# Routed experts at fitted widths, window attention in steps of two blocks, scores in bands of keys

## The chip, the core and the metric

The kernel runs on one NeuronCore of a Trainium2 chip. Its engines work side by side, each through its own queue in order: TensorE (PE; its weight loads are listed as PEld), VectorE (DVE), ScalarE (ACT), GpSimd (POOL) and SyncE (SP, which here only issues DMAs). The metric is the device time of one execution in microseconds; less is better.

## The reference

Two blocks follow each other, in float32. The first is attention with a local window and a few global keys: batch 4, 8 heads, 768 positions, head size 64.

```python
scores = scale * np.matmul(q, k.transpose(0, 1, 3, 2))
is_global = pos[None, :] < int(n_global)                 # n_global = 8
is_local = (rel >= 0) & (rel < int(n_local))             # n_local = 96
bias = -slopes[:, None, None] * dist[None, :, :]         # dist: distance, or n_local for a far global key
a = softmax(np.where(is_global | is_local, scores + bias, -1e9))
x = (a @ v) as 3072 tokens of 512 numbers                # heads side by side
```

The second sends each token to one of 8 experts (512 to 1024 to 512), the one whose embedding has the largest cosine with it, and weighs the result with that expert's probability.

```python
expert_idx = np.argmax(xn @ en.T / tau, axis=1)
for e in range(E):
    mask = expert_idx == e
    h = np.maximum(x[mask] @ w1[e], 0.0)
    out[mask] = gate_w[mask, None] * (h @ w2[e])
```

## The kernel before

Attention works on 8 groups (a batch and four of its heads, as two pairs `a` of two heads `e`). In a group the keys are cut into 8 blocks of 96; a unit is one block of keys with the 192 queries that can see it (the last: 96), and 30 rows of global keys ride along, so a score tile has 126 partitions. `score` (L329) multiplies keys by queries for four heads into two PSUM banks, takes one exponential of both banks on ACT (L341), and multiplies with a table of decays and masks on DVE (L347). `attend` (L349) runs one unit behind: v products (L367), and products with a matrix of ones that give the softmax denominators (L373), into three of four banks `od`; after four blocks they are copied to `xd`. Between them PE turns the next group's k and q (`turn`, L315) and works off one task of a list: `sums` (L398; logits of a tile of 128 tokens with the expert embeddings, L405, and transposes of denominators and of the last tile's logits) or `rows` (L425; transposes x, scales it, writes it to DRAM). `finish` calls `choose` (L145): the best expert, a token's rank within it by a matmul with a triangular matrix, its gate, and one small scatter for each tile of 128 tokens, which writes token number and gate to the expert's slots in DRAM (`meta`). The order of instructions on an engine is the scheduler's, from the order of the program.

The table (`window_table`, L236) is made at the start, from position tiles that POOL writes and numbers that are loaded by DMA.

The experts follow. `load_rows` (L626) reads 512 slots of an expert (it waits for all scatters), gathers their rows of x with four indirect DMAs; unused slots point at a row of zeros. `expert` (L648) transposes them (L655, copied by DVE, L656), takes the first product (L664: eight blocks of 128 hidden units, 512 columns of tokens), relu on ACT (L666), the second product (L671: four tiles of 128 tokens, 512 columns), scales by the gate (L674) and scatters rows to the output (L675). Every expert has 512 slots, however many tokens it has. Weights of the next expert load meanwhile into the other of two buffers. `leftover` (L681) handles what doesn't fit, behind a branch that isn't taken here (L699, L700).

## Time and profile before

| | us |
|---|---|
| median of three runs | 768.54 (766.0 to 772.91) |
| the profiled execution | 777.63 |
| its span, first to last instruction | 775.8 |
| PE busy in the span | 686.5 (88%) |
| DVE, ACT, POOL busy | 182.4, 147.6, 112.6 |
| granted PE clock, mean | 0.95 |

Busy times say how long an engine had an instruction in it; matmuls overlap, so a busy PE need not be a fast one. The granted clock is given as a share of 2.4 GHz; its two levels here are 1.0 and 0.5.

### The profile page before, as it was taken

Reading aid. Unit: us, or ns where it says so; the run is one execution under the profiler, and the core shown is the slowest. Engines: PE = TensorE matmul, PEld = TensorE weight load, DVE = VectorE, ACT = ScalarE, POOL = GpSimd, SP = SyncE. Lnnn points to the kernel's source line nnn. Section 1 sums busy time; section 2 is a strip of 40 time slices with the busy share of each in tenths; the row PEclk is TensorE's granted clock in tenths of the full one; section 3 lists DMA queues with packets and bytes.
Section 4 is the critical chain, followed back from the end, with each engine's and each line's share of the span. In section 5 each row is a group of like instructions: output and inputs, shape, how many; then the busy total and the mean of one; then the engine's idle time right before and its main releaser. Section 6 shows DMA issues by size and latency. Waiting matters only on the chain.

```text
span 775.8 us, 8382 instructions
## 1 busy us (share of the span) xinstructions
PE 686.5 (88%) x3394; PEld 353.0 (46%) x3394; DVE 182.4 (24%) x500; ACT 147.6 (19%) x280; POOL 112.6 (15%) x131
## 2 busy tenths in 40 slices
PE   4989986989799519999999999999999999999992
PEld 2556654555465304444444444444444444444440
DVE  2435562664366601011011011011011011011010
ACT  3545532543453200100100100100100100100100
POOL 2110022013003232012012012012012011010010
PEclk9999989898999758999999999999999999999996
DMA  9977669650110922214214115115114114000000
GB/s 185 213 129 213 177 177 39 137 118 7 37 42 16 283 48 90 83 58 174 81 53 171 78 71 175 71 64 172 64 70 168 64 77 146 0 37 14 0 26 18
DMA packets 99898, 74.57 MB, mean 96 GB/s; under 512 B 80762, under 2 KB 80890, under 8 KB 99850
## 3 DMA queue, kind: packets, MB, share of 16 engines
q1 hardware_dynamic: 90538, 58.44, 29.8%
q0 software_dynamic: 5888, 14.71, 5.4%
q10 hardware_dynamic: 3424, 0.79, 0.6%
q8 instruction: 29, 0.48, 0.3%
q14 instruction: 19, 0.16, 0.1%
HBM read 61.11 MB, written 14.90 MB: 98 GB/s over the span
## 4 chain that ended last, share of the span: by engine, by line
PE 59%; DVE 4%; DMA 3%; issue 0%; POOL 0%; SPq 0%; ACT 0%; DVEq 0%; ACTq 0%
PE big L664 29%; PE work L671 28%; DVE xT L656 2%; DMA x_dram<-xs 1%; DMA xg<-x_dram,ids 1%; DMA meta<-mt,slot 1%; DVE y L674 1%; PE tp L405 0%; PE tp L430 0%; PE tp L408 0%; DMA emt<-meta 0%; PE od L367 0%; PE work L655 0%; POOL out_dram L675 0%; SPq L630 0%
## 5 line engine op out<-in xcount | busy, mean ns | idle before, releaser
L664 PE MATMUL big<-xT,w1t 128*128 128x512 f32 x512 | 224.0, 598 | 11.2 <-DVE xT L656 11.2
L671 PE MATMUL work<-w2t,hT 128*128 128x512 f32 x512 | 221.0, 592 | 0.0
L664 PEld LDWEIGHTS big<-xT,w1t 128*128 128x128 f32 x512 | 97.4, 192 | 133.2 <-issue 120.0
L671 PEld LDWEIGHTS work<-w2t,hT 128*128 128x128 f32 x512 | 97.3, 190 | 122.5 <-issue 122.5
L674 DVE TENSOR_SCALAR y<-work,emt 128x512 f32<-128x512 f32 x32 | 24.0, 751 | 387.2 <-PE work L671 387.2
L666 ACT ACTIVATE hT<-big 128x1024 f32<-128x1024 f32 x32 | 32.8, 1023 | 432.0 <-PE big L664 432.0
L347 DVE TENSOR_TENSOR ex<-ex,table 126x384 f32<-126x384 f32 (+1 forms) x128 | 70.1, 585 | 89.0 <-ACT ex L341 89.0
L675 POOL DMA_INDIRECT out_dram<-y,ids x32 | 31.8, 995 | 337.8 <-DVE y L674 330.1
L337 PE MATMUL sp<-qT,kT 64*126 64x192 f32 (+1 forms) x512 | 66.8, 364 | 7.9 <-ACT qT L325 5.8
L367 PE MATMUL od<-ex,v 126*64 126x192 f32 (+1 forms) x576 | 62.6, 320 | 8.6 <-issue 4.6
L341 ACT ACTIVATE ex<-sp 126x768 f32<-126x768 f32 x64 | 49.1, 767 | 82.6 <-PE sp L337 60.8
L337 PEld LDWEIGHTS sp<-qT,kT 64*126 64x126 f32 x512 | 43.9, 196 | 28.1 <-issue 13.1
L367 PEld LDWEIGHTS od<-ex,v 126*64 126x64 f32 x576 | 34.1, 138 | 28.5 <-issue 18.6
L640 POOL DMA_INDIRECT xg<-x_dram,ids x32 | 30.9, 966 | 85.4 <-issue 42.9
L373 PE MATMUL od<-ex,ones 126*32 126x192 f32 (+1 forms) x576 | 36.3, 321 | 0.0
L655 PE MATMUL work<-ident,xg 128*128 128x128 f32 x128 | 17.7, 293 | 18.9 <-DMA xg<-x_dram,ids 18.9
L199 POOL DMA_INDIRECT meta<-mt,slot x24 | 23.8, 993 | 44.1 <-DVE slot L190 30.3
L655 PEld LDWEIGHTS work<-ident,xg 128*128 128x128 f32 x128 | 15.5, 151 | 23.7 <-DMA xg<-x_dram,ids 20.1
L320 PE MATMUL tp<-ident,k 128*128 128x128 f32 x96 | 19.7, 329 | 6.3 <-DMA k<-in_k_dram 6.0
L311 POOL COPY v<-v 30x1792 f32<-30x1792 f32 x8 | 13.6, 1698 | 74.8 <-DMA v<-in_v_dram 46.6
L430 PE MATMUL tp<-ident,xd 128*128 128x128 f32 x96 | 16.3, 298 | 8.2 <-DVE lh L420 6.3
L656 DVE COPY xT<-work 128x512 f32<-128x512 f32 x32 | 20.1, 682 | 6.8 <-PE work L655 6.5
(113 smaller groups left out, 297.4 us busy)
## 6 DMA issues: line engine op xcount, KB each, us to landing
w1t<-in_moe_w_dram SPq DMA_DIRECT2D x8, 2048.0 KB, 7.9
w2t<-in_moe_w_dram SPq DMA_DIRECT2D x8, 2048.0 KB, 10.8
k<-in_k_dram SPq DMA_DIRECT2D x32, 192.0 KB, 3.5
v<-in_v_dram SPq DMA_DIRECT2D x32, 192.0 KB, 4.5
x_dram<-xs SPq DMA_DIRECT2D x24, 256.0 KB, 6.3
q<-in_q_dram SPq DMA_DIRECT2D x28, 192.0 KB, 3.9
q<-in_q_dram ACTq DMA_DIRECT2D x4, 192.0 KB, 6.1
xg<-x_dram,ids POOLq DMA_INDIRECT x32
```

The source lines that it names most:

```text
L337: nc.tensor.matmul(sp[0:ROWS, e, a * n : (a + 1) * n], lhsT=t.kT[rows, j, 0:ROWS], rhs=t.qT[rows, j * BLK : j * BLK + n], start=True, stop ...
L341: nc.scalar.activation(ex, sp[0:ROWS, :, 0 : 2 * n], AF.Exp, scale=k.scale)
L347: nc.vector.tensor_tensor(out=exv, in0=exv, in1=tb, op=ALU.mult)
L367: nc.tensor.matmul(od[a][e * D : (e + 1) * D, cols], lhsT=g.v[0:ROWS, 2 * a + e, j, :], rhs=ex[:, e, a * n + c0 : a * n + c1], start=first ...
L373: nc.tensor.matmul(od[2][32 * i : 32 * i + 32, cols], lhsT=k.ones[0:ROWS, 0:32], rhs=ex[:, e, a * n + c0 : a * n + c1], start=first, stop= ...
L655: nc.tensor.transpose(ps[:, c, :], xgs[j][:, c * P : (c + 1) * P], k.ident[:])
L656: nc.vector.tensor_copy(out=xT[:, :, j * P : (j + 1) * P], in_=ps[:])
L664: nc.tensor.matmul(ps[:, i, :], lhsT=w1[:, c, f * P : (f + 1) * P], rhs=xT[:, c, :], start=c == 0, stop=c == k.NC - 1)
L666: nc.scalar.activation(hT[:, 2 * f2 : 2 * f2 + 2, :], ps[:], AF.Relu)
L671: nc.tensor.matmul(ps[:], lhsT=hT[:, f, j * P : (j + 1) * P], rhs=w2[:, f, :], start=f == 0, stop=f == k.NF - 1)
L674: nc.vector.tensor_scalar_mul(y[:], ps[:], mt[:, j, 1:2])
L675: nc.gpsimd.indirect_dma_start(out=k.out[:, :], out_offset=bass.IndirectOffsetOnAxis(ap=ids[:, j : j + 1], axis=0), in_=y[:], in_offset=No ...
```

## The change

In attention, a step is two units. Both units' scores come first on PE, then k and q of the next group, transposes of finished halves, and the v and ones products of the step before. Scores are computed in bands of 32 keys, each with the 128 queries that its keys can see, in 32-column strips of the array (`bands`); the exponential is taken for each bank (`grow`), the table multiplied once for a unit (`weigh`). PSUM is five rotating banks and three for `od`. Denominators of a batch's two groups are put in different columns by `halves` and added on DVE, so that they are turned once. Logits and their transposes are done for three tiles at once. The last two groups are interleaved by halves. The order on PE, ACT, DVE and SP is the program's (a manual schedule). Scatters of slots are held back and issued one or two in a step.

At the start, loads are split in halves in the order of use, the copies of global rows of group 0 come by DMA, an exponential loads ACT's table early, PE gets a few matmuls without use, and the table is made in two parts. Weights are loaded in 32 pieces an expert, in attention too, for experts 0 and 1.

Expert 0's first 256 slots, filled by the first three batches, are gathered three steps before the end (`first_rows`); their first product stands behind the last attention product, among the last router's work.

Each expert has a jump table of 13 arms, one for each width from 128 to 512 tokens in steps of 32 (`WIDTHS`). Only PE and ACT jump; the index comes from the counts (`choose_widths`). An arm holds the first product at that width, the whole tiles of 128 tokens of the second but the first, a left-over of 64 or 32 tokens in strips (`part_in_arm`), and the transposes of the next expert's rows. The jump's target is announced ahead (`switch_hint`), then a tile of the second product that every width has is done outside. Scatters of all tiles are issued in any case; those that a width lacks get row numbers out of range.

```diff
+WIDTHS = [128] + list(range(160, CAP + 1, 32))
...
+    for t in range(n):
+        nc.tensor.matmul(cp[:, (t + 1) * E : w + E], lhsT=k.ones[:],
+                         rhs=oh[:, t : t + 1, :].to_broadcast([P, n - t, E]), start=False, stop=True,
+                         skip_group_check=True)
...
     for m in range(2):
+        yield
...
+        bands = [(i * BAND, (i + 1) * BAND, i * BAND, min(i * BAND + BAND + BLK, n)) for i in range(BLK // BAND)]
+        bands.append((BLK, ROWS, 0, BLK))
...
+            for k0, k1, c0, c1 in bands:
+                for e in range(2):
+                    rows = slice(e * D, (e + 1) * D)
+                    nc.tensor.matmul(u.sp[e][k0:k1, a * n + c0 : a * n + c1], lhsT=t.kT[rows, j, k0:k1],
+                                     rhs=t.qT[rows, j * BLK + c0 : j * BLK + c1], start=True, stop=True,
+                                     skip_group_check=True)
...
+    def grow(u, e):
+        nc.scalar.activation(u.ex[:, e], u.sp[e][0:ROWS, 0 : 2 * u.n].rearrange("p (a c) -> p a c", a=2), AF.Exp,
+                             scale=k.scale)
+    def weigh(u):
+        kind = min(u.j, 2)
+        tab = k.table[0:ROWS, u.g.m].rearrange("p e a i c -> p (e a) i c")[:, :, kind::(3 - kind), :]
+        exv = u.ex.rearrange("p e a (i c) -> p (e a) i c", c=BLK)
+        nc.vector.tensor_tensor(out=exv, in0=exv, in1=tab[:, :, 0 : u.n // BLK, :], op=ALU.mult)
...
+    def attend(g, p):
+        if p % 2 == 0:
+            g.od = [po_p.tile([P, 512], F32, name="od%d" % i, tag="od%d" % i) for i in range(3)]
+        parts = []
+        if p == 2:
+            parts.append((g.units[3], 0, BLK, 2 * BLK, True))
+        for j in (2 * p, 2 * p + 1):
+            parts.append((g.units[j], (j % QB) * BLK, 0, BLK if j % QB == QB - 1 else 2 * BLK, j == 0))
...
+        if p % 2:
+            xd = xd_p.tile([P, 2, QB * BLK], F32, name="xd", tag="xd")
+            nc.scalar.copy(out=xd[:, 1, :], in_=g.od[1][:, 0 : QB * BLK])
+            nc.vector.tensor_copy(out=xd[:, 0, :], in_=g.od[0][:, 0 : QB * BLK])
+            g.xd.append(xd)
+            h, den = p // 2, g.batch.den
+            if g.m == 0:
+                den[h] = den_p.tile([P, QB * BLK], F32, name="den", tag="den")
+                nc.vector.tensor_copy(out=den[h][:], in_=g.od[2][:, 0 : QB * BLK])
+            else:
+                nc.vector.tensor_tensor(out=den[h][:], in0=g.od[2][:, 0 : QB * BLK], in1=den[h][:], op=ALU.add)
...
+    def turn_sums(hf):
+        t, h = hf.t, hf.h
         ps = bank()
+        for c in range(3):
+            nc.tensor.transpose(ps[:, c * P : (c + 1) * P], t.den[h][:, c * P : (c + 1) * P], k.ident[:])
...
+        for a in range(4):
+            nc.tensor.matmul(ps[32 * a : 32 * a + 32, 0 : 3 * P], lhsT=k.enb[:, a, :],
+                             rhs=t.groups[a // 2].xd[h][:, a % 2, :], start=True, stop=True)
...
+    def first_rows():
+        k.first = Net()
+        k.first.rows = load_rows(k, k.meta[0:FIRST, :], k.ea, k.ea2, FIRST // P, nc.gpsimd, k.ZR + 1)
...
+    def first_product(f):
+        if f % 2 == 0:
+            k.first.ps = bank()
+        ps = k.first.ps
+        for c in range(k.NC):
+            nc.tensor.matmul(ps[:, (f % 2) * FIRST : (f % 2 + 1) * FIRST], lhsT=k.w[0][0][:, c, f * P : (f + 1) * P],
+                             rhs=k.first.xT[:, c, :], start=c == 0, stop=c == k.NC - 1)
+        if f % 2:
+            nc.scalar.activation(k.first.hT[:, f - 1 : f + 1, :], ps[:].rearrange("p (i n) -> p i n", i=2), AF.Relu)
...
+    steps = [(g, p) for g in groups[: 2 * B - 2] for p in range(4)]
+    steps += [(g, p) for h in range(2) for g in groups[2 * B - 2 :] for p in (2 * h, 2 * h + 1)]
...
+    for s, (g, p) in enumerate(steps):
...
+        for u in us:
             score(u)
...
+        grow(us[0], 0)
+        grow(us[0], 1)
+        if s == 0:
+            next(table)
+        weigh(us[0])
+        scatter_later(k, 1 if s < len(steps) - 8 else 2)
+        grow(us[1], 0)
+        todo = [(x.pairs[a], i) for x, a, i in turns[s]]
+        if todo:
+            turn(*todo.pop(0))
+        grow(us[1], 1)
+        for x in todo:
+            turn(*x)
...
+        if s > 0:
+            q, qp = steps[s - 1]
+            attend(q, qp)
...
+        if s == len(steps) - 3:
+            scatter_later(k, len(k.later))
+            first_rows()
...
+    attend(*steps[-1])
+    for hf in active:
+        half_turns(hf)
+        half_router(hf)
+    scatter_later(k, len(k.later))
+    hf = start_half(t, 1)
+    score_experts(hf, bank())
+    first_turn()
+    turn_sums(hf)
+    xs = [turn_x(t, 3)]
+    turn_products(hf)
+    next(hf.router)
+    xs += [turn_x(t, 4), turn_x(t, 5)]
+    for i in range(3):
+        store_x(t, 3 + i, xs[i])
+    weights_part(len(weights))
+    first_product(0)
+    hf.router.send(bank()[:, 3 * P :])
+    next(hf.router)
+    next(hf.router)
+    scatter_later(k, len(k.later))
+    check_sums(t)
+    first_product(1)
+    for f in range(2, k.NF):
+        first_product(f)
...
+    mt = gp.tile([P, NJ, 3], F32, name="emt", tag="emt")
+    i = nc.sync.dma_start(mt[:], slots.rearrange("(j p) w -> p j w", p=P))
...
+def part_in_arm(k, t, hT, w2, base, size):
+    nc, n = k.nc, P // size
+    m = k.DM // n
+    ps = k.work.tile([P, k.DM], F32, name="work", tag="work")
+    for f in range(k.NF):
+        for i in range(n):
+            nc.tensor.matmul(ps[i * size : (i + 1) * size, 0:m], lhsT=hT[:, f, base : base + size],
+                             rhs=w2[:, f, i * m : (i + 1) * m], start=f == 0, stop=f == k.NF - 1)
+    nc.scalar.mul(t.y_part[size][:], ps[:, 0:m], t.parts[size][1][:])
...
+def first_by_eight(k, xT, w1, hT, w, between=None):
+    nc = k.nc
+    for f in range(k.NF):
+        ps = k.big.tile([P, CAP], F32, name="big", tag="big")
         for c in range(k.NC):
+            nc.tensor.matmul(ps[:, 0:w], lhsT=w1[:, c, f * P : (f + 1) * P], rhs=xT[:, c, 0:w],
+                             start=c == 0, stop=c == k.NC - 1)
+        nc.scalar.activation(hT[:, f, 0:w], ps[:, 0:w], AF.Relu)
+        if between:
+            between(f)
...
+    def between(f):
+        for j in {5: (0,), 6: (1, 2), 7: (3,)}.get(f, ()) if coming else ():
+            turn_row(k, coming.rows, coming.xT, j, k.nc.scalar.copy)
+    tiles = range(0 if behind else 1, CAP // P)
+    for arm in tc.Switch(now.width.index, len(WIDTHS), hint=now.width.hint):
+        w = WIDTHS[arm]
+        first_by_eight(k, now.xT, w1, hT, w, between)
+        for size in (64, 32):
+            if w % (2 * size) >= size:
+                part_in_arm(k, now, hT, w2, w // (2 * size) * 2 * size, size)
+        for j in tiles:
+            if j < w // P:
+                second_in_arm(k, now, hT, w2, j)
+    if coming:
+        coming.width = take_width(k, coming.e)
+    def scatters():
+        for j in tiles:
+            scatter_rows(k, now.y[:, j, :], now.tile_ids[:, j : j + 1])
+        for size in (64, 32):
+            scatter_rows(k, now.y_part[size][:], now.parts[size][0][:], P // size)
+    out = [scatters]
+    if behind:
+        behind(out)
+    else:
+        second(k, now.rows, hT, w2, 0, k.work0, out)
...
+    v = k.nc.values_load(k.pick[0:1, e : e + 1], engines=ARMS, min_val=0, max_val=len(WIDTHS) - 1)
+    t.index, t.hint = {eng: v for eng in ARMS}, "expert%d" % e
+    k.tc.switch_hint(t.index, len(WIDTHS), t.hint)
...
+            choose_widths(n)
+            coming = numbers(0)
+            prepare(coming)
+            coming.width = take_width(n, 0)
+            second(n, n.first.rows, n.first.hT, n.w[0][1], 0, n.work)
...
+            for e in range(n.E):
+                now, coming, after = coming, after, None
+                if coming:
+                    prepare(coming)
+                for scatter in pending:
+                    scatter()
+                if e + 2 < n.E:
+                    after = numbers(e + 2)
+                    split_rows(n, after)
+                behind = None
+                if e == 0:
+                    def behind(out):
+                        second(n, n.first.rows, n.first.hT, n.w[0][1], 1, n.work0, out)
+                pending = expert(n, now, coming, behind)
```

## Rows read from the trace of the kernel before

**Rows 1.** The page: busy tenths of PE in 40 equal slices of the span.

```profile
PE   4989986989799519999999999999999999999992
```

**Rows 2.** Windows by stage: us; busy PE, PEld, DVE, ACT, POOL; PEclk; DMA; GB/s.

```profile
0.00:21.30 21.30, 8.07 (x28) 5.42 (x28) 5.23 (x20) 8.55 (x19) 5.63 (x22) 1.00 1.07 188
21.30:254.30 233.00, 209.14 (x2162) 130.70 (x2162) 120.87 (x340) 102.84 (x219) 36.32 (x37) 0.94 0.55 108
254.30:294.06 39.76, 13.28 (x73) 9.17 (x66) 14.25 (x73) 3.44 (x12) 14.86 (x17) 0.58 0.55 171
294.06:760.50 466.44, 456.00 (x1138) 207.73 (x1138) 40.91 (x65) 32.75 (x32) 54.76 (x56) 1.00 0.23 82
760.50:775.80 15.30, 0.05 (x1) 0.00 (x0) 1.17 (x4) 0.00 (x0) 0.98 (x1) 0.57 0.06 18
```

**Rows 3.** Chain of waits, expert 1 and its next: start us, us, what.

```profile
354.61 27.73 PE big L664 x64
382.34 27.48 PE work L671 x64
...
413.05 27.73 PE big L664 x64
```

**Rows 4.** Timeline of PE, one steady unit: start us, us, instructions.

```profile
211.92 0.43 PE L405 MATMUL tp<-xd,enb 128*32 128x128 f32 x8
212.27 0.44 PE L408 MATMUL tp<-ident,xd 128*128 128x128 f32 x2
...
212.75 0.87 PE L367 MATMUL od<-ex,v 126*64 126x192 f32 x8
213.55 0.53 PE L373 MATMUL od<-ex,ones 126*32 126x192 f32 x8
214.01 0.92 PE L337 MATMUL sp<-qT,kT 64*126 64x192 f32 x8
214.86 0.55 PE L320 MATMUL tp<-ident,k 128*128 128x128 f32 x3
215.25 0.60 PE L430 MATMUL tp<-ident,xd 128*128 128x128 f32 x4
215.78 0.55 PE L367 MATMUL od<-ex,v 126*64 126x96 f32 x8
```

**Rows 5.** PE's waits in attention: for whom, us, times, longest.

```profile
PE tp L430 <- DVE lh L420: 6.3, 1, 6.3
...
PE od L367 <- issue: 4.6, 3, 4.0
```

**Rows 6.** Windows around an idle stretch of PE, columns as in rows 2.

```profile
42.20:45.40 3.20, 0.30 (x9) 0.09 (x9) 1.53 (x4) 1.09 (x3) 0.99 (x3) 1.00 0.31 71
45.70:49.20 3.50, 3.50 (x17) 2.65 (x15) 0.19 (x1) 2.21 (x5) 2.09 (x3) 0.51 0.44 101
```

**Rows 7.** Timeline of the start, PE and ACT.

```profile
5.96 1.51 PE L320 MATMUL tp<-ident,k 128*128 128x128 f32 x6 [5.96 <-DMA k<-in_k_dram]
...
17.49 3.41 ACT L274 ACTIVATE table<-rel 128x384 f32<-128x384 f32 x8 [3.85 <-DVE rel L270]
...
21.32 1.01 PE L337 MATMUL sp<-qT,kT 64*126 64x192 f32 x4 [5.78 <-ACT qT L325]
```

**Rows 8.** Groups by shape, exponentials on ACT: busy us, mean ns, idle before.

```profile
L341 ACT ACTIVATE ex<-sp 126x768 f32<-126x768 f32 x56 | 45.3, 808 | 74.5 <-PE sp L337 58.3 <-remote 8.2 <-issue 3.3
...
L341 ACT ACTIVATE ex<-sp 126x384 f32<-126x384 f32 x8 | 3.8, 477 | 8.1 <-remote 5.6 <-PE sp L337 2.5
```

**Rows 9.** Chain of waits, the hole before the experts.

```profile
275.59 6.05 DMA meta<-mt,slot
...
284.91 6.25 DMA xg<-x_dram,ids x2
```

**Rows 10.** L699 and L700, PE sequencer: ns least/median/most, starts us.

```profile
L699 PEldq TENSOR_LOAD <-fi x1: 492/492/492, 761.8 to 761.8; - x1
...
L700 PEldq COMPARE_BRANCH  x1: 4402/4402/4402, 762.4 to 762.4; - x1
```

More of the change, by code (lines that the diff above doesn't have):

```diff
@@ L41, in build_consts @@
     nc.vector.memset(k.ones[:], 1.0)
+    k.halves = pool.tile([P, 2, 2, 16], F32, name="halves")
+    nc.vector.memset(k.halves[:], 0.0)
+    for m in range(2):
+        nc.vector.memset(k.halves[:, m, m, :], 1.0)
 def build_route_consts(k):
@@ L208, in choose, with scatter_later @@
             k.scatters.append(i.ins)
+    k.later.extend((scatter, t) for t in range(n))
+    if k.scatters is None:
+        scatter_later(k, n)
+    yield
+def scatter_later(k, n):
+    for scatter, t in k.later[:n]:
+        scatter(t)
+    del k.later[:n]
 def route(k, b, xb, pool):
@@ L369, in attend @@
                                      skip_group_check=True)
+        for u, at, c0, c1, first in parts:
             for a in range(2):
@@ L460, in window_attention @@
+    groups = [new_group(b, m) for b in range(B) for m in range(2)]
     for g in groups:
+        g.units = []
         for j in range(NB):
@@ L463, in window_attention @@
             u.g, u.j, u.n = g, j, (2 * BLK if j < NB - 1 else BLK)
[L464 to L477 removed]
+            u.late = g.b == B - 1 and j == QB - 1
@@ new lines, in window_attention @@
+            g.units.append(u)
+    first = groups[0]
+    open_group(first)
+    numbers = load_numbers(k, k.n_global, k.n_local)
+    build_consts(k)
+    for a in range(2):
+        load_tokens(nc.sync, first.pairs[a].k, k.k, 0, a, 0, 3)
+        load_tokens(nc.scalar, first.pairs[a].q, k.q, 0, a, 0, 3)
+    next(numbers)
+    warm = const.tile([P, 1], F32, name="warm")
+    nc.scalar.activation(warm[:], k.ones[:, 0:1], AF.Exp)
+    for a in range(2):
+        load_tokens(nc.sync, first.pairs[a].q, k.q, 0, a, 3, NT)
@@ new lines, in window_attention, with busy @@
+    for a in range(2):
+        load_tokens(nc.sync, first.pairs[a].k, k.k, 0, a, 3, NT)
+    for ps in banks:
+        nc.vector.memset(ps[:], 0.0)
+    idle = bank()
+    def busy(n):
+        for _ in range(n):
+            nc.tensor.matmul(idle[:, 0:64], lhsT=k.ones[:], rhs=k.ones[:, 0:64], start=True, stop=True)
+    busy(8)
+    load_v(first, range(4))
+    emb = prep_expert_emb(k, k.emb_in, k.tau, tmp)
+    next(emb)
+    open_group(groups[1])
+    for p in range(4):
+        load_part(groups[1], p)
@@ L518, in window_attention @@
-    while tasks:
-        tasks.pop(0)()
+    table = window_table(k, tmp)
+    next(table)
+    next(numbers)
+    next(table)
+    check_numbers(k)
+    build_route_consts(k)
+    steps = [(g, p) for g in groups[: 2 * B - 2] for p in range(4)]
+    steps += [(g, p) for h in range(2) for g in groups[2 * B - 2 :] for p in (2 * h, 2 * h + 1)]
+    turns = [[] for _ in steps]
+    turn(first.pairs[0], 0)
+    turn(first.pairs[0], 2)
+    busy(3)
+    turn(first.pairs[1], 0)
+    turn(first.pairs[1], 2)
@@ new lines, in expert @@
+def expert(k, now, coming=None, behind=None):
+    tc = k.tc
+    w1, w2 = now.w
+    hT = k.hp.tile([P, k.NF, CAP], F32, name="hT", tag="hT")
+    if coming:
+        coming.xT = k.xtp.tile([P, k.NC, CAP], F32, name="xT", tag="xT")
+    def between(f):
[21 more added lines that the diff above has]
+        behind(out)
+    else:
+        second(k, now.rows, hT, w2, 0, k.work0, out)
+    return out
```

758 lines of the change are left out of this document (476 added, 282 removed).

## The prediction, made before the change was run

> **What bounds the kernel now.** I read the page's strip of forty slices first: TensorE (PE) reads 9 in nearly all of them, with one hole between 250 and 300 us and a smaller one at the start [rows 1]. A busy PE is a share, not a limit, so next come the windows cut at four events: first steady score, last attention product, first expert matmul, last expert matmul [rows 2]. They give five stages: start 21.3 us, attention 233.0, a hole of 39.8 between attention and experts, experts 466.4, drain 15.3. In the expert stage the chain of waits is PE alone: 64 matmuls of the first product take 27.73 us, 64 of the second 27.48, and the next expert begins 58.44 us after the last, so 3.2 us go to transposes and their copies [rows 3]. That stage is bound by columns streamed: every expert is padded to 512 tokens. In the hole the chain is DMA latency and routing arithmetic, with PE mostly idle. Attention needs the order of PE in one steady unit [rows 4].
>
> **What one unit costs on PE.** Start to start in [rows 4]: expert logits (8 instructions of 128 columns, four column strips) 0.35 us, v products (8 of 192 columns, two strips) 0.80, ones products (8 of 192, four strips) 0.46, scores (8 of 192, two row halves) 0.85, three transposes 0.39, four 0.53. An f32 matmul is two instructions here. Strips run side by side: v is four rounds, ones two, and their difference, 0.34 us, is two rounds of 192 columns; so a round is 0.17 us (0.113 for 128 columns) and each change of strip pattern costs about 0.12 (0.17 for scores). The logits check this: 2 x 0.113 + 0.12 = 0.35. A unit is 0.85 + 0.80 + 0.46 + 0.39 = 2.50; 64 units are 160 us, and 24 token tiles with logits, sums and x rows at about 1.4 bring it to some 199 with routing. The stage took 233. The other 34 are PE idle in the list of PE's waits (its longest are DVE's logits, 6.3, and "issue", 4.6 [rows 5]) and half clock: 0.94 granted over 233 us [rows 2] is 28 us at 1.2 GHz, and [rows 6] show how it comes: PE nearly idle from 42.2 to 45.4, then the clock at 0.51 for the next 3.5 us though PE was busy throughout.
>
> **Start: 21.3 to about 9 us.** The first score waited for a copy queued on ScalarE (ACT) behind eight table exponentials, which ran from 17.49 [rows 7]. Those waited for position tiles that GpSimd (POOL) made behind a copy of v. The change sends group 0's global rows by DMA, loads halves in the order of need, makes the position tiles first and cuts the table in two, its first half after the first exponential. The first three-tile halves are 0.79 MB; at the stage's 188 GB/s [rows 2] that is 4.2 us; the first transposes run at 5.96 now [rows 7], and twelve of them with their copies end near 9. The DMA share there is already 1.07 [rows 2], so groups 0 and 1 (4.7 MB and the broadcast) are in by about 27 us and steps 1 to 3 wait some 6 us; that is in the stalls below.
>
> **Attention: 233 to about 185 us.** A step has two units. Scores in bands: three bands of 32 keys see 128 queries each (a key needs only its 96 and its band), the global rows 96, in 32-column strips and two row halves. That is 64 instructions for a step instead of 16. Eight strips side by side make 8 rounds of 0.113 + 0.17 = 1.08 us, against 1.70 now. No row shows eight together; rows show two and four [rows 4]. I take eight, since both patterns pack fully; the far bounds are four together, 16 x 0.113 + 0.17 = 1.98, and the logits' 0.044 us an instruction as if issue were the limit, 2.8. v products of two units follow each other without a change of pattern: 8 x 0.17 + 0.12 = 1.48; ones 4 x 0.17 + 0.12 = 0.80; six transposes 0.78. A step is 4.14, 32 are 132. For each half batch 18 transposes (sums of both groups are added first, so three, not six) at 0.13 and logits of 384 columns (2 x 0.34 + 0.12) make 3.1, eight are 25; six routers with one ones-matmul a tile, about 8. Sum 165. To it come 20 us of stalls: the start's 6, and 14 of the 34 now. The lag of a whole step between weighing and attending takes away waits such as the 6.3 us one; code fetch may grow, since 24 matmuls and as many weight loads a unit, 3,000 instructions, are added on PE and "issue" waits are there already. Bounds 8 to 40.
>
> ACT and VectorE (DVE) don't take over: ACT was busy 102.8 us here, DVE 120.9 [rows 2]. An exponential per bank costs 2 x 0.477 for 0.808 [rows 8], so ACT gains 64 x 0.15 = 9 us, to 112. DVE's two multiplies become one. Both stay far under 165. What is queued on PE behind a late exponential is a whole step, so such a wait would show at once.
>
> **The hole: 39.8 to about 34 us.** The chain now is routing, the last scatter's landing (6.05, at 281.6), the slots' reading (gathers start at 284.9), gathers (6.25 for two) [rows 9], transposes. The change leaves each link and shortens the front: three token tiles remain after the last product instead of up to six, one chain of logits. Step by step (copies 0.6, logits 0.8, copy 0.5, transposes, DVE sums 0.8, choice 1.1, x rows 2.1, squares, power, slots) I get the slots at +11 us, the last scatter issued at +15, landed at +21, slots read at +24, gathers and copies done at +34. Slots are read as 512 pieces of 12 bytes instead of 128 of 32: up to a microsecond more, counted. Under this cover PE does expert 0's first 256 rows, gathered three steps earlier: 64 instructions of 256 columns, 13.9 us, and one tile of the second product, 6.87. If the cover went, those 21 us would stand in the expert stage. POOL's queue holds the first half's three scatters ahead; it was busy 14.9 of the 39.8 us [rows 2], so they are out before the slots come. Bounds 28 and 40.
>
> **Experts: 466.4 to about 341 us.** The reference's own routing of its seeded inputs sends 406, 310, 510, 319, 322, 369, 472 and 364 tokens; 315 of expert 0's come in the first three batches, so 256 are taken early and 150 remain. Rounded up, the widths are 160, 320, 512, 320, 352, 384, 480, 384, together 2,912 columns instead of 4,096. First product: 27.73 x 2912 / 512 = 157.7. Second: 20 whole tiles in the widths and expert 0's second early tile, 21 x 6.87 = 144.3. Left-over strips: 64 rows four times, 32 instructions of 256 columns in two strips, 16 x 0.227 + 0.12 = 3.75, 15.0 together; 32 rows three times, 16 x 0.113 + 0.12 = 1.93, 5.8 together. If strips didn't overlap they would cost 7.3 and 7.2 each, 30 us more. Transposes of the coming expert now stand inside the arm: 28 x 4 x 0.13 = 14.6, with no wait for DVE. Each expert adds a register load (0.49 [rows 10]) and a jump in and out on PE and ACT. The only jump that the trace has, at the end, held PE's sequencer for 4.40 us [rows 10]. Here the target is announced before 6.87 us of outside matmuls that are already queued, so I take 0.5 a jump pair and keep 8.8 as the bound. POOL's ten indirect DMAs an expert, 0.98 us each now (54.8 for 56 [rows 2]), lie under 26 to 57 us of matmuls, and weights of 4 MB likewise. Sum 157.7 + 144.3 + 20.8 + 14.6 + 4 = 341.4.
>
> **Drain** as now, 15.3: five scatters of the last arm go out beside the outside tile.
>
> **Sum against the profiled execution.** 9 + 185.5 + 34 + 341.4 + 15.3 = 585.2 against a span of 775.8; 1.8 lies around the span, 587. The profiled execution of 777.63 stands 1.2% above the median of 768.54; the same ratio gives 580.
>
> The Trainium skill, "Runtime: NRT & Kernel Launch", Instruction fetch mechanics, says that a taken branch whose target is outside what is loaded waits for its code to come by DMA. By that rule the arms would cost what the second rival says; the trace agrees with it at the final jump (4.40 us) and shows no announced one.
>
> **Rivals.**
> Bands pack only four wide, or are limited by issue: for it, no row with eight. It gives 32 x 0.9 = 29 us more, 609; by the logits' pace 32 x 1.7 = 55, 635. Chance 0.20. The Trainium skill, "TensorE: Matmul & The Clock Gate", Wait — 56ns, not 53.3ns?, gives a floor of about 25 ns from one matmul's start to the next; an estimate by it is 64 x 0.025 = 1.6 us a step, 597 in all, while rows go no lower than 44 ns.
> Jumps are not covered: 16 x 4.4 = 70 us, 650. For it the final jump, against it the announced target and the queue ahead of it. Chance 0.08.
> Slower: each break at an arm leaves PE at 1.2 GHz, as after the idle in [rows 6], and the whole expert stage stays there. Its 337 us of streaming then double, 913. It turns the sign once over 56% of them, (768.5 - 580) / 337, run at half clock. Against it: 1.00 over all eight experts now [rows 2], with a 3.2 us gap at each. Chance 0.01.
> The change doesn't do what it says, every expert picks 512: 124 us more, 704. The counts speak against it. Chance 0.01.
> Better than summed: eight strips pack, stalls fall to 8, the hole to 28: 560 or a little under. Chance 0.12.
> Forecast: 0.58.
>
> **Range and chances.** The low end, 550, is the last case with a shorter start; the high end, 640, takes in narrow bands and half the jump loss. A change under 1% can't be told from none here. All cases but one lie far below: faster 0.97, within 1% 0.01, slower 0.02.
>
> **What would show it.** First steady score near 9 us; 32 steps near 5.5 us with eight score instructions starting within one round; last attention product near 195; first arm's matmuls near 229; PE gaps under 1 us at the jumps; outside-tile-to-outside-tile times that follow the widths, from 27 us (expert 0) to about 57 (expert 2); last matmul near 570. The sum is wrong if PE waits for ACT in each step, if the granted clock falls in the arms, or if PE's code comes late.

## The result, and the profile after

The changed kernel takes 593.1 us at the median of four runs (584.05 to 595.8) beside 769.87 for the kernel before (766.0 to 772.91): ratio 0.7644, 95% interval 0.7579 to 0.771. The ratio is not that of the two medians (0.7704): of the four runs it leaves out the two that lie over 1.5% above the fastest, 594.41 and 595.8, and takes in two more, 587.35 and 590.24. Forecast were 580, range 550 to 640. A second series of six runs gave 587.78 (584.86 to 593.75), ratio 0.7619 (0.7582 to 0.7656); the experiments are compared with that one. The profiled execution took 584.05 us, its span 582.1.

The page's strip of forty slices for TensorE in the changed kernel, to be laid beside [rows 1]:

```profile
PE   8889999999898978999999999999999999999920
```

The hole in the middle is gone from this strip, and at its end two slices are nearly empty where it was one. The same five windows as in [rows 2], same columns, changed kernel:

```profile
0.00:11.00 11.00, 8.51 (x40) 8.39 (x40) 6.28 (x24) 3.98 (x8) 4.16 (x28) 1.00 0.77 161
11.00:184.40 173.40, 161.95 (x3623) 124.24 (x3626) 110.04 (x253) 106.43 (x281) 46.30 (x49) 0.96 0.83 176
184.40:219.70 35.30, 29.26 (x139) 21.02 (x132) 13.26 (x61) 6.43 (x15) 11.75 (x12) 0.94 0.53 132
219.70:556.72 337.02, 336.07 (x1280) 184.46 (x1281) 40.18 (x204) 57.33 (x112) 71.28 (x73) 1.00 0.34 116
556.72:582.10 25.38, 0.28 (x3) 0.19 (x1) 1.20 (x4) 0.00 (x0) 3.91 (x4) 0.57 0.05 14
```

| stage, us | before | forecast | after |
|---|---|---|---|
| start | 21.3 | 9 | 11.0 |
| attention | 233.0 | 185.5 | 173.4 |
| hole | 39.8 | 34 | 35.3 |
| experts | 466.4 | 341.4 | 337.0 |
| drain | 15.3 | 15.3 | 25.4 |
| span | 775.8 | 585.2 | 582.1 |

The experts give two thirds of the gain, attention nearly a third. The drain, the stretch behind the last expert matmul, grew, and with the attention it is what the forecast missed most. The hole lasts nearly as long as before, but TensorE is busy in 29.26 of its 35.3 us, where it was busy in 13.28 of 39.76.

TensorE's timeline of one steady step of the changed kernel, to set beside the unit in [rows 4]:

```profile
62.55 1.13 PE L454 MATMUL pa<-qT,kT 64*32 64x128 f32 x64
63.60 0.55 PE L429 MATMUL pa<-ident,k 128*128 128x128 f32 x3
63.99 0.49 PE L429 MATMUL pa<-ident,q 128*128 128x128 f32 x3
64.31 0.60 PE L553 MATMUL pa<-ident,xd 128*128 128x128 f32 x4
64.75 0.49 PE L520 MATMUL pa<-ident,den 128*128 128x128 f32 x3
65.17 1.20 PE L481 MATMUL od<-ex,v 126*64 126x192 f32 x16
66.30 0.70 PE L489 MATMUL od<-ex,halves 126*32 126x192 f32 x16
66.82 0.83 PE L529 MATMUL pa<-xd,enb 128*32 128x384 f32 x8
67.58 1.13 PE L454 MATMUL pa<-qT,kT 64*32 64x128 f32 x64
...
101.84 1.13 PE L454 MATMUL pa<-qT,kT 64*32 64x128 f32 x64
```

A bracket would show time that TensorE stood idle before a row; there is none in this step. The next work starts 1.05 us after the step's 64 score instructions (62.55 to 63.60), 16 ns an instruction; 1.08 was forecast from rows that showed two and four strips. From 62.55 to 101.84 are eight steps, 39.3 us.

TensorE's timeline across two experts of the changed kernel:

```profile
242.00 7.03 PE L968 MATMUL work<-w2t,fhT 128*128 128x512 f32 x16
248.87 13.08 PE L1066 MATMUL big<-xT,w1t 128*128 128x320 f32 x48
...
278.52 7.03 PE L968 MATMUL work<-w2t,hT 128*128 128x512 f32 x16
285.38 4.88 PE L1066 MATMUL big<-xT,w1t 128*128 128x512 f32 x11
```

The outside tile (the tile of the second product that stands behind the arm) and the next arm's first matmul follow each other without a gap, at 320 and at 512 columns. From outside tile to outside tile it is 36.5 us for expert 1 here.

### The profile page after: what moved, and what is told of

Read it like the earlier page. It is cut to its first block, busy times and chain, and to the rows that moved or that the text cites. A ratio compares the mean times of both kernels' runs of the same rounds, so it can differ in the third digit from the quotient of the medians.

```text
span 582.1 us, 12322 instructions
## 1 busy us (share of the span) xinstructions
PE 536.1 (92%) x5078; PEld 338.3 (58%) x5078; DVE 171.0 (29%) x543; ACT 174.2 (30%) x416; POOL 137.4 (24%) x166
## 5 line engine op out<-in xcount | busy, mean ns | idle before, releaser
L1066 PE MATMUL big<-xT,w1t 128*128 128x320 f32 (+5 forms) x512 | 161.7, 473 | 0.8 <-DVE xT L959 0.8
L1035 PE MATMUL work<-w2t,hT 128*128 128x512 f32 x208 | 91.1, 595 | 0.0
L1068 ACT ACTIVATE hT<-big 128x320 f32<-128x320 f32 (+5 forms) x64 | 30.4, 474 | 186.7 <-PE big L1066 186.7
L466 DVE TENSOR_TENSOR ex<-ex,table 126x768 f32<-126x768 f32 x64 | 59.4, 931 | 47.6 <-ACT ex L459 44.4
L1035 PEld LDWEIGHTS work<-w2t,hT 128*128 128x128 f32 x208 | 39.0, 190 | 47.5 <-issue 46.2
L1054 POOL DMA_INDIRECT out_dram<-y_arm,tids x25 | 24.8, 992 | 172.5 <-ACT y_arm L1037 103.5
L459 ACT ACTIVATE ex<-pa 126x384 f32<-126x384 f32 (+1 forms) x128 | 53.5, 478 | 21.8 <-PE pa L454 21.2
L968 PE MATMUL work<-w2t,hT 128*128 128x512 f32 x112 | 49.2, 592 | 0.0
L454 PE MATMUL pa<-qT,kT 64*32 64x128 f32 (+3 forms) x2048 | 38.5, 269 | 0.9 <-DVE xs L562 0.4
L454 PEld LDWEIGHTS pa<-qT,kT 64*32 64x32 f32 (+1 forms) x2048 | 30.2, 107 | 12.1 <-issue 6.5
L968 PEld LDWEIGHTS work<-w2t,hT 128*128 128x128 f32 x112 | 21.3, 190 | 26.8 <-issue 26.8
L404 POOL COPY v<-v 30x896 f32<-30x896 f32 x14 | 15.6, 1120 | 54.0 <-DMA v<-in_v_dram 15.3
L489 PE MATMUL od<-ex,halves 126*32 126x192 f32 (+1 forms) x576 | 27.2, 313 | 0.0
```

Of the source, the lines that this page charges most:

```text
L454: nc.tensor.matmul(u.sp[e][k0:k1, a * n + c0 : a * n + c1], lhsT=t.kT[rows, j, k0:k1], rhs=t.qT[rows, j * BLK + c0 : j * BLK + c1], start= ...
L459: nc.scalar.activation(u.ex[:, e], u.sp[e][0:ROWS, 0 : 2 * u.n].rearrange("p (a c) -> p a c", a=2), AF.Exp, scale=k.scale)
L466: nc.vector.tensor_tensor(out=exv, in0=exv, in1=tab[:, :, 0 : u.n // BLK, :], op=ALU.mult)
L489: nc.tensor.matmul(g.od[2][32 * i : 32 * i + 32, at : at + c1 - c0], lhsT=k.halves[0:ROWS, g.m].rearrange("p i c -> p (i c)"), rhs=u.ex[:, ...
L968: nc.tensor.matmul(ps[:], lhsT=hT[:, f, j * P : (j + 1) * P], rhs=w2[:, f, :], start=f == 0, stop=f == k.NF - 1)
L1035: nc.tensor.matmul(ps[:], lhsT=hT[:, f, j * P : (j + 1) * P], rhs=w2[:, f, :], start=f == 0, stop=f == k.NF - 1)
```

## The experiments

**How far two series agree.** The changed kernel again, unaltered.

> The changed kernel once more, as the measure for the others of its group: both theories expect a ratio of 0.764 (0.758 to 0.771) to the kernel before.

587.78 us, as said above. Its profile has the stages 11.0, 177.4, 34.3, 337.2, 25.6. So attention differs by some 4 us between two profiles of one kernel, the experts by 0.2. The experiments below that leave attention as it is widen this: over eight profiles with the same attention it took 171.7 to 178.5 us, and the hole 34.3 to 40.8. Between two profiles a difference of a few us in either stage says nothing.

**The widths.** Every expert takes the arm of 512.

```diff
+    nc.vector.tensor_scalar(out=pick[:], in0=pick[:], scalar1=0.0, scalar2=float(V - 1), op0=ALU.mult, op1=ALU.add)
```

> Every expert takes the arm of 512 tokens: the index of the arm is set to the last one on VectorE after it is worked out; everything else stays. This gives the worth of the fitted widths alone. By the prediction's terms: the first product is 8 x 27.73 = 221.8 us less expert 0's early 256 columns (13.9) = 208 instead of 157.7 (+50; expert 0's arm still skips the early slots where it did before); whole tiles in the arms rise from 20 to 30 or so (+72), strips fall from 20.8 to 0. The prediction put the whole at +124 and the time at 704. Theory (PE is the bound through the whole expert stage, so widths count in full): +95 to +125 us against the changed kernel, 683 to 713, ratio to the kernel before 0.885 to 0.925. Rival (the jumps and the arms' structure, not the widths, carry the gain, or padded weights and gathers hide): less than +60, under 650.

712.5 us (706.78 to 714.18), ratio 0.9228 (0.9163 to 0.9292): 124.7 us more. The window of its expert stage:

```profile
222.20:683.80 461.60, 461.60 (x1152) 210.02 (x1153) 38.66 (x192) 68.86 (x117) 71.35 (x73) 0.99 0.26 85
```

461.6 against 337.0 us: all of the difference lies in this stage, and TensorE is busy in every microsecond of it. With all arms at 512 the stage is only 4.8 us shorter than before the change (466.4), though it holds one tile (6.87) more, so arms and jumps as such bring little; the columns were the time. The 124.7 us aren't the widths alone, though: expert 0's arm runs at 512 columns here too (the stage has 512 instructions of that width in the first product, 64 an expert), although 256 of its slots were done ahead of it. My expectation had it skip them. Some 28 of the 124.7 us, an estimate from the prediction's terms (256 columns 13.9, two tiles 13.7), are the worth of taking those rows early, some 97 that of the fitted widths.

**The announced target.**

```diff
-    k.tc.switch_hint(t.index, len(WIDTHS), t.hint)
+    t.hint = None
```

> The jump target isn't announced. Theory: what covers a jump is that PE's sequencer runs ahead of the array by several us (the outside tile's 6.87 us are queued when it branches), so even an unannounced jump, at the 4.4 us of the final one, leaves PE gaps under 1 us and the time grows by less than 5 us (under 1%). Rival: the announcement is what covers it; then eight entries cost 4.4 us each, 35 us more, ratio 0.81, with a PE gap of 3 to 5 us ahead of each first product.

588.99 us (584.03 to 590.45), ratio 0.763 (0.7593 to 0.7667): no difference. The expert stage stays at 337.0 us and TensorE has no gap in it. Expert 0's arm, at the cut between hole and experts, is the one with little queued ahead of it: transposes that wait for the gathers. TensorE's timeline at its first product, changed kernel, then without the announcement:

```profile
219.69 8.15 PE L1066 MATMUL big<-xT,w1t 128*128 128x160 f32 x48 [0.79 <-DVE xT L959]
```

```profile
225.68 9.55 PE L1066 MATMUL big<-xT,w1t 128*128 128x160 f32 x48 [3.24 <-DVE high L1016]
```

The branch into this arm took 1.32 us in the one, ending at 219.43, and 3.75 in the other, ending at 225.40; there it is what the product waits for, whatever engine the bracket names. That the announcement makes the difference isn't shown: of the eleven profiles with it, eight have this branch at 0.45 to 1.32 us, but three at 2.8 to 3.3 with gaps of 2.9 to 3.2; the two without it have 3.75 and 3.34.

**The tile outside the arm.** Both kernels have `tiles = range(CAP // P)` in the arm, and experts 1 to 7 lose the tile behind it; the second also drops the announcement.

```diff
-    tiles = range(0 if behind else 1, CAP // P)
+    tiles = range(CAP // P)
...
-    else:
-        second(k, now.rows, hT, w2, 0, k.work0, out)
```

> The tile of the second product that every width has moves from outside into the arm, for every expert but 0 (whose early tile stays); the announcement of the target stays, now just before the jump. PE's work is the same. Since dropping the announcement cost nothing, the theory is that the 6.87 us of matmuls queued ahead cover the jump: without them each of seven jumps shows a PE gap of 2 to 6 us between the experts (the dispatch branch took up to 6 us on PE's sequencer), 14 to 42 us together, and the drain grows by up to 7 us because all scatters of the last expert follow its arm: 605 to 635. Rival (jumps are cheap by themselves, or the announcement is enough): no gap over 1 us between experts, only the drain's growth, 588 to 597.

> As the kernel without the outside tile, and the targets are not announced either. Theory (only queued matmuls cover a jump; an announcement just ahead of it comes too late to help): the same as without the outside tile alone, within 5 us. Rival (the announcement is what makes the jump short when nothing is queued): 2 to 5 us more in each of seven jumps, 14 to 35 us above the kernel without the outside tile alone.

596.5 us (593.22 to 601.38) with the announcement, 599.88 (598.85 to 602.09) without. Their expert stages take 340.6 and 340.1 us, 3 more than the changed kernel's, and their drains 31.2 and 30.9, 6 more. My expectation of 2 to 6 us a jump fell: with the announcement five of the seven jumps show gaps, 2.0 us together. TensorE's timeline where the gap was largest, kernel without the outside tile, then without both:

```profile
365.90 14.00 PE L1035 MATMUL work<-w2t,hT 128*128 128x512 f32 x32
380.83 3.49 PE L1066 MATMUL big<-xT,w1t 128*128 128x352 f32 x11 [0.93 <-issue]
```

```profile
372.55 14.00 PE L1035 MATMUL work<-w2t,hT 128*128 128x512 f32 x32
387.91 4.38 PE L1066 MATMUL big<-xT,w1t 128*128 128x352 f32 x14 [1.37 <-issue]
```

The jump itself is not cheap. The branches of TensorE's sequencer in the changed kernel and in the one without tile and announcement (ns least/median/most; half of the 16 leave an arm, half enter one):

```profile
L1369 PEldq COMPARE_BRANCH  x16: 312/1981/6023, 218.1 to 542.1; - x16
```

```profile
L1367 PEldq COMPARE_BRANCH  x16: 311/3228/7626, 223.8 to 559.8; - x16
```

In the trace of the changed kernel the branch into expert 4's arm starts at 371.35 and ends at 377.30; the array is busy until 378.58. Without the outside tile, but with the announcement, it runs from 373.96 to 380.57, and the array is done at 379.9. In both the sequencer is 6 to 7 us ahead of the array, because matmuls are queued; whether they belong to the arm or to a tile outside makes no difference to that. A branch of some 6 us fits just inside the lead with the outside tile and sticks out by up to 1.4 us without it.

**The early work in the hole.** The kernel leaves out expert 0's early first product and first early tile; zeros stand for the hidden values.

```diff
-    first_product(0)
+    nc.gpsimd.memset(k.first.hT[:], 0.0)
...
-    first_product(1)
-    for f in range(2, k.NF):
-        first_product(f)
...
-            second(n, n.first.rows, n.first.hT, n.w[0][1], 0, n.work)
```

> Leaves out expert 0's early first product (64 matmuls of 256 columns, 13.9 us of PE by the prediction) and its first early tile of the second product (6.87 us); the hidden values of these slots are zeros, so that expert's rows come out wrong. The slots' reading, the gathers and the router stay. Theory (both lie under the latency chain of the hole: scatter landing, slots, gathers): the time stays within 4 us of the changed kernel's 588, and the stretch from the last attention product to the first arm stays 33 to 38 us with PE idle for about 20 of it; possibly 2 to 4 us more, since PE then stands idle and begins the experts at the low granted clock. Rival (the hole is bound by PE's work, not by the chain): 13 to 21 us less, 567 to 575, and the hole falls under 25 us.

588.67 us (584.97 to 590.68), ratio 0.7617 (0.7572 to 0.7662): the 20.8 us of matmuls gone, the time the same. The window of its hole:

```profile
188.60:225.90 37.30, 10.74 (x58) 8.04 (x54) 11.74 (x58) 4.15 (x11) 10.75 (x11) 0.61 0.48 125
```

TensorE's busy time in the hole falls from 29.26 to 10.74 us, and the hole doesn't shrink, so TensorE's work doesn't bind it. The chain of [rows 9] does: in the trace of the changed kernel the last scatter of slots is issued 15 us after the last attention product and lands at 21, the slots are read at 23, the last gather lands at 33, and TensorE waits for it:

```profile
217.82 1.09 PE L958 MATMUL work<-ident,xg 128*128 128x128 f32 x4 [1.01 <-DMA xg<-x_dram,ids]
```

Without the early products the granted clock of the hole has a mean of 0.61 instead of 0.94.

**Bands.**

```diff
-        bands = [(i * BAND, (i + 1) * BAND, i * BAND, min(i * BAND + BAND + BLK, n)) for i in range(BLK // BAND)]
-        bands.append((BLK, ROWS, 0, BLK))
+        bands = [(0, ROWS, 0, n)]
```

> Scores again for all 126 key rows at once, 192 queries, two row halves side by side; all else as changed. By the rounds of the prediction a step's scores go from 1.05 us to 8 x 0.17 + 0.17 = 1.5 to 1.7, so attention grows by 32 x 0.45 to 0.65 = 14 to 21 us and the ratio by 0.02 to 0.027. Rival: attention is held by ACT and by waits, not by PE, and PE had slack in each step; then the time moves by less than 5 us.

588.58 us (586.88 to 591.78), ratio 0.7638 (0.7595 to 0.7681): no difference (to within some 4 us by the intervals, where 14 to 21 more were expected), so my theory fell. The steady step with whole scores, first and eight steps later:

```profile
64.45 1.57 PE L453 MATMUL pa<-qT,kT 64*126 64x192 f32 x16
65.95 0.55 PE L429 MATMUL pa<-ident,k 128*128 128x128 f32 x3
...
106.08 1.24 PE L453 MATMUL pa<-qT,kT 64*126 64x192 f32 x11
```

Scores take 1.26 to 1.50 us a step, not twice the 0.85 of [rows 4]: two units in one go pay the change of pattern once. Eight steps last 41.6 us instead of 39.3, so bands do save 0.3 us a step. The window of the attention, once for all instructions and once for the score line alone, whole scores; then the score line in the changed kernel:

```profile
11.00:188.30 177.30, 167.50 (x2087) 132.00 (x2090) 109.46 (x254) 107.10 (x281) 44.70 (x49) 0.99 0.82 172
...
11.00:188.30 177.30, 49.79 (x512) 40.83 (x512) 0.99 0.82 172
```

```profile
11.00:184.40 173.40, 38.48 (x2048) 30.16 (x2048) 0.96 0.83 176
```

Scores are busy for 11.3 us less with bands, TensorE as a whole for 5.5 less (161.95 against 167.50), the stage 3.9 shorter, or 0.1 longer in the second profile of the changed kernel. The other 5.8 us of busy time came back in other products: the same v products hold TensorE, from each start to the next, for 48.1 us with bands and 45.2 with whole scores. The clock column has room for that: 0.96 against 0.99 is 14 us at 1.2 GHz against 3.5, some 5 us of work. All nine profiles with bands throughout and the written order lie at 0.94 to 0.97. Why it falls more often with bands isn't shown.

**The written order.** First with bands, then with whole scores:

```diff
-        with tc.manual_schedule(engines=ORDERED), ExitStack() as inner:
+        with ExitStack() as inner:
```

> The attention part loses its manual schedule: the same instructions are emitted, but the scheduler chooses the order on PE, ACT, VectorE and SyncE again, as in the kernel before; the expert part keeps its written order. Attention took 173 to 177 us in the changed kernel, 155 of it the steps' own work (8 steps take 38.9 us where they run steadily) and 18 to 22 of stalls, half clock and a slow start. Theory (the steps' own work, with sums turned once and logits for three tiles at once, carries the gain, and a step's lag leaves the order some room): attention grows by stalls only, 5 to 20 us, total 593 to 608. Rival (the written order carries it): attention returns toward the 233 us of before, 30 us or more, total over 615. Third case (the scheduler finds as good an order): within 3 us, 585 to 591.

> Attention without the written order (the scheduler's order again) and with whole scores instead of bands, 16 score instructions in a step instead of 64. With bands and the scheduler's order the attention took 220.2 us, and from one PE start to the next the scores took 73.8 us of it against 38.5 in the changed kernel: the scheduler cuts the 64 instructions of a step into pieces of 16 to 46 between other work. Theory (the loss is that cutting: bands need the eight strips next to each other): whole scores lose less, scores 50 to 60 us, attention 195 to 206, total 600 to 612. Rival (the order matters as such: waits and half clock, whatever the scores' shape): attention 215 to 225, total 620 to 632, no better than with bands.

627.61 us (625.36 to 632.87), ratio 0.8075 (0.8005 to 0.8144), and 618.2 (614.73 to 621.43), ratio 0.8021 (0.7964 to 0.8077). The first, like the next experiment, was measured beside a kernel before of 780.25 us, so ratios are compared. The attention takes 220.2 and 206.3 us. The order is worth 0.0456 of the time before with bands, 35 us, and 0.038 with whole scores, 30 us, each to within some 6 us. TensorE's timeline of the kernel with bands in the scheduler's order:

```profile
86.16 0.40 PE L454 MATMUL pa<-qT,kT 64*32 64x128 f32 x2
86.50 0.55 PE L429 MATMUL pa<-ident,k 128*128 128x128 f32 x3
86.97 0.41 PE L454 MATMUL pa<-qT,kT 64*32 64x128 f32 x6
87.61 0.77 PE L454 MATMUL pa<-qT,kT 64*32 64x128 f32 x24 [0.23 <-ACT kT L431]
88.86 0.55 PE L429 MATMUL pa<-ident,k 128*128 128x128 f32 x3 [0.48 <-ACT ex L459]
89.34 1.27 PE L454 MATMUL pa<-qT,kT 64*32 64x128 f32 x32
```

Two score instructions cost 0.34 us before the next work starts, 32 cost 1.21, where 64 in one block cost 1.05. The score lines of the two kernels over their attention, bands and then whole:

```profile
11.20:231.40 220.20, 63.38 (x2048) 40.45 (x2048) 0.95 0.67 149
```

```profile
11.00:217.30 206.30, 65.22 (x512) 49.84 (x512) 0.98 0.73 159
```

For the kernels with bands it is 63.38 us against 38.48 for the same 2,048 instructions. I had thought that bands alone suffer from being cut; whole scores rise as well, from 49.79 to 65.22, so that part fell. The last run's total, 618.2, lies between its two forecasts, its attention at the upper edge of the theory's; its scores, 70.3 us by the expectation's measure from start to start, are near the 73.8 with bands and far from the 50 to 60 of the theory. Scores aren't all of it: of the 47 us that attention grows by with bands they make 35, from start to start, and v products 9. The Trainium skill, "TensorEngine Tiling (Array Packing)", Key Properties, says that a change of tiling mode drains the array; these pieces agree with it, though no run here counts the changes.

**Transfers in the middle of attention.**

```diff
-        def weights_part(n=1):
+        def weights_part(n=2):
...
-                if s >= 6 and weights:
+                if s >= 16 and weights:
```

> The weight pieces of expert 0 start at step 16 instead of step 6, four in a step instead of two; the rest stays. This takes 4 MB out of the middle of attention, where the DMA share is 0.9 to 1.0 between 40 and 140 us, and puts it later. Theory (the middle of attention is bound by PE's own stream, not by transfers): the eight steps from about 58 us stay at 38.7 to 39.3 us, and the total stays within 4 us of 588. Rival (whole scores and bands come out alike because transfers bind): the steps before step 16 get shorter, 36 us or less for eight, and the time falls by 3 to 8 us.

590.38 us (588.78 to 596.03), ratio 0.7597 (0.7529 to 0.7665). The DMA share between 56 and 96 us falls from 0.96 to 0.76, and eight steps from 56.1 us take 39.7: no shorter. The transfers don't bind there. Put later they lengthen the steps near the end (attention 185.3 us) and the hole is 31.7.

**The output scatters.** They are declared independent of each other, as the scatters of slots are already.

```diff
-    k.nc.gpsimd.indirect_dma_start(
+    i = k.nc.gpsimd.indirect_dma_start(
...
+    if k.outs is not None:
+        if k.outs:
+            k.tc.declare_no_dep(i.ins, group="outs", reason="rows are distinct")
+        k.tc.add_to_no_dep_group("outs", i.ins)
+        k.outs.append(i.ins)
```

> The trace of the changed kernel shows each output scatter starting 2 to 3 us after the one ahead of it, when that one has landed, so the last six need 15.6 us from the first start to the last (551.02 to 566.59). Here the scatters are declared independent. If the drain grew from 15.3 to 25.4 us for that reason, the last six start 1.3 us apart, the last at about 558.3 (it still needs the outside tile, whose scaling ends at 557.7), and the drain falls to about 17 us: 8 us less, a ratio 0.010 lower. The rival, that POOL's own work for a scatter is 3 us, expects no change in the spacing and none in the time.

582.16 us (579.77 to 583.93), ratio 0.7548 (0.7517 to 0.7578), against 587.78 on the same chip. GpSimd's timeline at the end of the changed kernel, and of this one:

```profile
551.02 0.98 POOL L1054 DMA_INDIRECT out_dram<-y_arm,tids  x1 [26.07 <-ACT y_arm L1037]
554.14 0.98 POOL L1054 DMA_INDIRECT out_dram<-y_arm,tids  x1 [2.15 <-DMA out_dram<-y_arm,tids]
...
562.74 0.98 POOL L1054 DMA_INDIRECT out_dram<-y,pids  x1 [2.39 <-DMA out_dram<-y,pids]
566.59 0.98 POOL L1054 DMA_INDIRECT out_dram<-y,ids  x1 [2.87 <-DMA out_dram<-y,pids]
```

```profile
556.42 0.98 POOL L1054 DMA_INDIRECT out_dram<-y_arm,tids  x1 [33.33 <-ACT y_arm L1037]
557.71 0.98 POOL L1054 DMA_INDIRECT out_dram<-y_arm,tids  x1 [0.30 <-issue]
...
561.56 0.98 POOL L1054 DMA_INDIRECT out_dram<-y,pids  x1 [0.30 <-issue]
563.35 0.98 POOL L1054 DMA_INDIRECT out_dram<-y,ids  x1 [0.81 <-DVE flags L1179]
```

In the brackets of the changed kernel each scatter waits for the landing of the one before, 2.3 to 3.9 us apart; freed, they follow at 1.28. The last, for the outside tile, starts 9.9 us after the last matmul in the one and 1.25 in the other. The drain falls from 25.4 to 19.2 us, 3.9 more than before the change. What is left lies behind the last scatter. GpSimd's closing DRAIN before the change, and with free scatters:

```profile
L819 POOLq DRAIN  x3: 40/107/7266, 767.7 to 775.6; - x3
```

```profile
L1374 POOLq DRAIN  x3: 46/107/8897, 571.5 to 581.0; - x3
```

This is 1.6 us of the 3.9, and the DRAIN takes 8.8 to 8.9 us in all profiles of the changed kernel and its variants. Another 1.6 us is the stretch from the last scatter's start to the end of GpSimd's waits, 5.8 us instead of 4.3; with free scatters it ends where that scatter lands. Why the two are longer isn't shown.

**Both together.** Free scatters, and whole scores in the last eight steps only:

```diff
+        if whole:
+            bands = [(0, ROWS, 0, n)]
...
-            score(u)
+            score(u, s >= 24)
```

> Output scatters independent of each other, as in the run with free scatters, and in addition the last eight steps (the two interleaved groups) compute whole scores, with bands in the 24 steps before. In the changed kernel bands shorten eight steady steps from 41.6 to 38.9 us, but the last eight steps with the last attention products took 42.5 to 48.6 us with bands (46.3 on average) against 44.3 with whole scores. Theory (bands leave PE waiting for the router's VectorE work near the end and then at the low clock, so their saving is given back there): attention 2 us shorter than with bands throughout, 172 to 175; with the freed scatters 578 to 583 in all, ratio 0.750 to 0.757. Rival (the differences of the last steps are scatter from run to run): attention as before, 174 to 178, total 581 to 585.

583.3 us (577.76 to 585.47), ratio 0.7481 (0.7431 to 0.753) to a kernel before that took 780.25 us beside it, 1% more than elsewhere. Its profile has an attention of 180.8 us, no shorter, so the theory on the last steps fell. Against free scatters alone it is undecided.

## Why the prediction was right, and where it was off

The likeliest case held: bound by TensorE's columns in the expert stage, by the order of its work in attention, by latency in the hole. The 580 is 2.2% under the first median and 1.3% under the second, although the span was forecast 0.5% too long: the profiled execution of before stood 1.2% above its median, that of after below, so the factor for it pointed the wrong way. That the total came so near is in part luck: attention was put 12.1 us too long, the drain 10.1 too short, and the two nearly cancel.

**Start**, 11.0 for 9: right in kind.

**Attention**, 173.4 for 185.5. The "Sum 165" was mis-sized, the stalls were not. Eight steady steps take 39.3 us, 38.9 in the second profile, where my terms make 8 x 4.14 + 2 x 3.1 + 2 = 41.3; four times the measured step group is 156 to 157, and 16 us, or 22 in the second profile, are left for stalls, half clock and the slow first steps (20 were forecast). I priced every v and ones product at 192 columns. In the steady step above one of the two units has 96, and v takes 1.13 us instead of 1.48, ones 0.52 instead of 0.80; one step in four has a third piece of 96 columns and gives part of that back. Over the eight steps, from start to start, v takes 11.0 us instead of 11.8 and ones 5.8 instead of 6.4, which is most of the 2.0 us. The scores' 1.08 held. The rival of four strips fell, and so did the floor taken beside it from the Trainium skill, "TensorE: Matmul & The Clock Gate", Wait — 56ns, not 53.3ns?: 16 ns an instruction are measured where 25 were estimated by that page.

What brought the gain was not split by the prediction as the runs split it. It put 0.62 us a step on the bands (1.70 to 1.08), 20 us; they save 11.3 us of scores, and nothing that the total shows, because whole scores for two units in one go are cheap too. It gave the written order no price of its own: 30 to 35 us hang on it. The rest, down from 233 to some 206 without order and bands, belongs to the other edits together, which weren't tried one by one.

**Hole**, 35.3 for 34 (34.3 to 40.8 in other profiles of the same code), link by link as forecast: slots out at +15, landed at +21, read at +23 for +24, gathered and copied at +35 for +34. The cover named for the 20.8 us of early work is the right one: leaving it out changes nothing.

**Experts**, 337.0 for 341.4. The rival in which every expert picks 512 was put at 124 us more, and 124.7 were measured; both contain expert 0's early rows. The 4 us for jumps are the term that was too large: no gap at the jumps of experts 1 to 7, while the one into expert 0's arm stands in the hole. The step "announced before 6.87 us of outside matmuls" named two covers. The queue is the one that counts there, and matmuls of the arm itself nearly do for it; the announcement shows nothing in the time. The rule from the Trainium skill, "Runtime: NRT & Kernel Launch", Instruction fetch mechanics, that a taken branch to code that isn't loaded waits for it, agrees with the sequencer's 6 us at an arm; it costs nothing there because the array lags by 7.

**Drain**, 25.4 for 15.3, the step that failed: "as now, 15.3: five scatters of the last arm go out beside the outside tile". I counted them as issues beside 6.87 us of matmuls and overlooked that the program orders writes to one tensor, so that each waits for the landing of the one before. Before the change a scatter comes every 6.87 us and waits for its own rows alone, as GpSimd's timeline of that kernel shows:

```profile
754.63 0.98 POOL L675 DMA_INDIRECT out_dram<-y,ids  x1 [5.89 <-DVE y L674]
```

Freeing them gives back 6.2 of the 10.1 us. The other 3.9 lie behind the last scatter, in its landing and in GpSimd's closing DRAIN, where the forecast took "as now".

## What to carry to other kernels

Price a run of like matmuls by where its tiling pattern changes, not by its columns alone: here a written order, which among other things keeps a step's 64 narrow matmuls in one block, was worth 30 to 35 us, and making them narrow nothing that the total shows. A branch cost TensorE nothing here while matmuls that lasted longer than the branch were queued ahead of it; look for the branch on the sequencer and the gap on the array separately, and look at the first branch too, which may have nothing queued. When an edit puts several scatters to one tensor behind each other, look whether each waits for the one before, and say so to the scheduler if their rows are distinct.

## What the hardware showed unexpectedly

Sixty-four f32 score instructions in eight strips run in 1.05 us, 16 ns each, while the same instructions cut into pieces take 0.34 us for two. TensorE's sequencer ran 6 to 7 us ahead of the array, enough to hide a branch of 6. With the early products left out, TensorE was busy for 10.74 us of the hole instead of 29.26 and the hole's mean granted clock was 0.61 instead of 0.94, at no cost in time.
